# Zero fills on another engine, shorter decay loads, one more order condition and a new order table in a gated-recurrence plus feed-forward kernel

## The chip, the cores and the metric

The kernel runs on one core of a Trainium2 chip. The metric is the device time of one execution in microseconds (us), the median of several runs. The core has TensorE (PE in the profile; PEld is its weight load), VectorE (DVE), ScalarE (ACT), GpSimd (POOL) and SyncE (SP), which here only issues DMA transfers. TensorE's clock has two levels, 1.2 and 2.4 GHz; the profile gives the granted clock as a share of the upper one.

## The reference

Two stages follow each other. The first is a recurrence over 768 time steps for 4 batches of 8 heads of width 40; the second is a feed-forward layer with a rational activation. Weights of the second stage arrive as 64-bit floats.

```python
for t in range(S):                       # S = 768, per batch and head
    m_new = max(f[t] + m, i[t])
    f_stab, i_stab, m = exp(f[t] + m - m_new), exp(i[t] - m_new), m_new
    C = f_stab * C + i_stab * outer(v[t], k[t])
    n = f_stab * n + i_stab * k[t]
    y[t] = sigmoid(o_gate[t]) * (C @ q[t]) / max(abs(n @ q[t]), 1)
x = y as (3072, 320)
h = x @ w_in                             # 320 -> 2048
g = (a0 + a1*h + a2*h*h + a3*h**3) / (1 + |b0|*|h| + |b1|*h*h + 1e-6)
out = g @ w_out                          # 2048 -> 320
```

## The kernel before

The recurrence is computed in chunks of 64 steps. A *unit* u handles 128 steps (two chunks) of one batch with its eight heads: 24 units. A *block* n of the feed-forward layer takes the 256 tokens of units 2n and 2n+1 (tile `xk`), and runs in eight *stages* i, each over 256 of the 2048 hidden columns: 12 blocks, 96 stages.

For a unit, SP loads the keys and queries (`ld`: tiles `kr` and `qn`), the values (`lv`: `vb`), and the gate factors from scratch memory (`lg`: `fb` and `ab`). `ab` holds the cumulated decays, the same row copied to 64 + 64 partitions. Then `kp` scales the keys (POOL), `tk` transposes them (PE, first transposes), `ek` copies them out (ACT), `tq` transposes the queries (PE, second transposes), `eq` copies them out (ACT), `qa` multiplies them with `ab` (DVE), `S` forms the scores (PE), `sc` builds the decay matrix `e` (DVE), `P` and `ke` apply it, `ow` forms the sums that update the state (PE), `u0` and `u1` update the states `sm` and `st` (DVE) with `d0` and `d1` (POOL) before them, `it` and `i1` form the output in PSUM tile `y`, and `ab`, `rc`, `g`, `x`, `xt`, `xh`, `xl` normalise it, gate it and write it transposed into `xk`.

A feed-forward stage is `f1` (PE, PSUM tile `ph`), `ha`, `p1`, `u`, `y`, `r0` on ACT, `p3`, `gh`, `m`, `gl` on DVE, `w` and `rm` on POOL, and `f2`, `f3` on PE (PSUM tile `po`, from `gH` and `gL`). Before that the 64-bit weights are loaded in 18 slabs (`raw`: names j0, j1 for the last 64 rows of `w_in`, i0 to i7 for the rest of it, o0 to o7 for `w_out`) and turned into two 32-bit parts: `s0` (ACT), `s1` (DVE), `s0`, `s1`, `o0` (ACT), `o2` (POOL).

At the start the gate factors of the first two chunks are computed on DVE (`early`, tiles `early_e`, `early_kT`, `early_qA`), stored to scratch, and read back by `lg`; those of all other chunks follow (`gates`). Some tiles must be zero where no load writes them: `kp`, `vb0`, `qn0` and `qb` are cleared before the branch on the flag, and `qn1`, `vb1`, `sm`, the four `st` and half of `wY` in `setup`. PE is given 90 products of the identity (`hot`) to do where nothing else is ready.

The order on each engine is fixed when the kernel is built. Every step is added to a planner with an order key, and the planner takes on each engine, among the steps whose inputs are there, the one with the lowest key. It assumes a cost for each step, and 2.75 us from the end of an issue to the landing of a load. A unit's key is

```python
base = 2 * u - LEAD + (UNIT_AT[u] if u < len(UNIT_AT) else 0.0)
key = base + ATT_AT[name] + LOAD_AT[u]      # LOAD_AT for SP's steps of units 0 to 7
```

and for a weight slab with number `key` in the order j0, i0, o0, i1, o1, j1, i2, o2, i3, o3, ...

```python
at = PREP_AT[op] + PREP_AT["step"] * key + SLAB_AT[key] + (PREP_AT["out"] if name[0] == "o" else 0.0)
```

to which `NUDGE` adds a number of its own for single steps. Each engine then runs its list in order: an instruction that waits holds up all behind it on its engine, SP's list included. A condition in the planner (`r`, `w`) between steps of the same engine fixes their order and is no wait on the chip.

Of the kernel before, what the change touches and what calls it, by code (L numbers as in the profile page):

```python
# [189 lines left out]
BLOCK_AT = (-30.05, -20.9)  # L190
# [11 lines left out]
    o0_i3=-86.73, o2_i3=-68.16, raw_o3=-30.6, s0_o3=-86.83, s1_o3=-112.32, o0_o3=18.04, o2_o3=-97.03,
    raw_i4=-20.87, s0_i4=19.22, s1_i4=-143.2, o0_i4=21.48, o2_i4=-312.68, s0_o4=-160.32, s1_o4=0.96, o0_o4=3.24,
    raw_i5=-8.26, s0_i5=-110.61, s1_i5=-96.8, o0_i5=-137.56, o2_i5=-81.65, raw_o5=34.48, s0_o5=-123.6,
    s1_o5=-133.73, o0_o5=25.43, o2_o5=-182.58, raw_i6=-62.5, s0_i6=-109.42, o0_i6=-14.16, o2_i6=-230.79,
    s0_o6=2.67, s1_o6=-71.7, o0_o6=44.51, o2_o6=-403.32, raw_i7=5.23, s0_i7=-13.29, s1_i7=-238.6, o0_i7=39.05,
    o2_i7=-23.84, raw_o7=-36.78, s0_o7=3.25, s1_o7=-198.97, o2_o7=-67.4, ogl_0=-0.03, og_0=3.41, ld_0=-6.33,
    lg_0=11.88, lv_0=12.65, kp_0=100.21, sc_0=50.31, tk_0=915.2, ek_0=-1.35, tq_0=997.06, eq_0=-0.9,
    qa_0=138.15, S_0=40.63, ke_0=-15.75, P_0=11.71, ow_0=914.85, u0_0=-0.64, i1_0=-94.1, u1_0=-5.16,
    rc_0=137.27, g_0=87.1, x_0=113.44, xt_0=949.12, xh_0=106.04, lg_1=201.84, lv_1=181.76, kp_1=123.51,  # L210
    sc_1=-6.49, tk_1=936.74, ek_1=20.81, eq_1=20.85, qa_1=55.87, ke_1=25.86, P_1=179.55, it_1=24.11, u0_1=7.7,
    d1_1=89.23, u1_1=4.5, ab_1=77.75, rc_1=45.19, g_1=-14.56, x_1=-19.25, xt_1=971.3, xh_1=138.71, xl_1=64.48,
    ogl_3=1.48, ogl_4=3.6, ogl_5=1.54, og_2=-50.77, ld_2=139.07, lg_2=182.61, lv_2=-82.51, kp_2=116.69,
    sc_2=99.12, tk_2=909.8, ek_2=123.31, tq_2=991.7, eq_2=118.94, qa_2=34.83, S_2=-21.68, ke_2=-12.55,
    P_2=-1.16, it_2=921.63, u0_2=11.63, d1_2=-128.57, i1_2=-79.84, u1_2=108.87, rc_2=25.69, g_2=-133.39,
    x_2=123.07, xt_2=-44.66, xh_2=-33.5, xl_2=54.23, lg_3=-0.89, lv_3=252.92, kp_3=93.7, sc_3=-10.43,
    tk_3=-65.69, tq_3=15.48, eq_3=0.4, qa_3=152.51, S_3=1.34, ke_3=-23.2, P_3=157.11, ow_3=-66.94, it_3=-56.07,
    u0_3=151.6, d1_3=85.48, i1_3=945.59, u1_3=178.13, g_3=15.21, x_3=146.78, xt_3=41.5, xh_3=197.9,
    xl_3=-210.89, ld_4=112.13, lg_4=157.92, lv_4=117.27, kp_4=101.03, sc_4=136.18, ek_4=144.46, eq_4=-3.95,
    qa_4=-17.72, S_4=-2.95, ke_4=-73.28, P_4=-50.56, d0_4=-6.47, ow_4=-11.6, it_4=-1.13, u0_4=-51.89,  # L220
    d1_4=27.44, i1_4=-0.94, u1_4=22.81, rc_4=-145.43, g_4=71.53, x_4=97.04, xt_4=72.26, xh_4=201.32, xl_4=69.51,
# [1086 lines left out]
```

## Time and profile before

| | |
|---|---|
| median of 3 runs | 573.15 us (570.04 to 574.14) |
| the profiled execution | 573.32 us |
| its span, first to last instruction | 571.4 us |
| around the span | 1.92 us |
| PE, DVE, ACT, POOL busy | 526.4, 475.8, 430.8, 394.3 us |
| mean granted clock of PE | 0.959 |

The profile follows one execution on each engine. Busy time is time in which an engine has an instruction under way, a wait for a memory port included. Idle time before an instruction is put down to what ended it (after `<-`). Helper functions record every instruction of the program at line 34, so tiles name the work.

### The profile page before, as it was taken

To read this page: it belongs to the slowest core of one execution; us is meant where nothing else is said; L and a number is where in the kernel's file an instruction comes from. 1 tells how busy PE (TensorE), PEld (TensorE's weight loads), DVE (VectorE), ACT (ScalarE), POOL (GpSimd) and SP (SyncE) were. 2 spreads that over 40 slices of the span, in tenths; PEclk is the share of its full clock that TensorE was granted. 3 is DMA by queue.
4 is the path that set the end of the run, shared out by engine and by line. 5 is a ranking of instruction groups with operands and counts; after the bars stand their busy time and mean duration, and the time that the engine had idled before them with its cause. 6 is when DMAs were issued, how large, how long until landed. Compare 5 with 4: busy or idle time off the path is not lost.

```text
span 571.4 us, 13096 instructions
## 1 busy us (share of the span) xinstructions
PE 526.4 (92%) x5024; PEld 492.9 (86%) x5024; DVE 475.8 (83%) x782; ACT 430.8 (75%) x757; POOL 394.3 (69%) x353
## 2 busy tenths in 40 slices
PE   4956796899999999999999999999999999999994
PEld 4955676799989999999999898899899999999993
DVE  8979898997888779987888877877987878878684
ACT  2647689886866888777788868888877777778982
POOL 4536669996687697777868684586777686757762
PEclk9967597999999999999999999999999999999998
DMA  5799877422331323333313214232122010000000
GB/s 168 173 241 243 227 171 157 89 62 58 91 67 45 64 50 77 65 72 77 78 38 85 36 50 97 64 66 73 35 64 70 13 36 2 1 26 1 23 1 30
DMA packets 120666, 44.10 MB, mean 77 GB/s; under 512 B 103826, under 2 KB 113106, under 8 KB 120594
## 3 DMA queue, kind: packets, MB, share of 16 engines
q1 hardware_dynamic: 120594, 43.18, 33.2%
q8 instruction: 41, 0.67, 0.5%
q14 instruction: 31, 0.25, 0.1%
HBM read 39.03 MB, written 4.13 MB: 76 GB/s over the span
## 4 chain that ended last, share of the span: by engine, by line
PE 68%; DVE 11%; POOL 6%; issue 4%; DMA 3%; ACT 3%; SPq 3%; DVEq 0%; POOLq 0%; ACTq 0%
PE ph L34 27%; PE po L34 25%; PE y L34 6%; PE ps L34 4%; PE kq L34 3%; PE ow L34 2%; DVE w L34 2%; DVE gH L34 2%; POOL p L34 2%; DVE gL L34 1%; ACT ph L34 1%; POOL tm L34 1%; PE px L34 1%; DMA rawj<-in_moe_w_in_dram 1%; DMA rawo<-in_moe_w_out_dram 1%
## 5 line engine op out<-in xcount | busy, mean ns | idle before, releaser
L34 POOL TENSOR_TENSOR p<-p,w 128x512 f32<-128x512 f32 (+1 forms) x97 | 128.7, 1327 | 85.0 <-DVE w L34 78.3
L34 PE MATMUL ph<-xk,wi 128*128 128x256 f32 x1152 | 173.8, 286 | 0.9 <-DVE gL L34 0.7
L34 POOL TENSOR_TENSOR w<-w,ha 128x512 f32<-128x512 f32 (+1 forms) x97 | 138.4, 1427 | 34.9 <-ACT w L34 31.0
L34 PEld LDWEIGHTS ph<-xk,wi 128*128 128x128 f32 x1152 | 151.9, 188 | 5.9 <-issue 1.9
L34 PE MATMUL po<-wo,gH 128*128 128x320 f32 x768 | 135.8, 315 | 1.8 <-DVE gH L34 1.8
L34 PEld LDWEIGHTS po<-wo,gH 128*128 128x128 f32 x768 | 114.9, 188 | 4.8 <-DVE gH L34 2.6
L34 DVE SCALAR_TENSOR_TENSOR gH<-p,ps,ph 128x512 fp32r<-128x512 f32 (+1 forms) x97 | 71.6, 738 | 34.0 <-PE po L34 15.3
L34 DVE SCALAR_TENSOR_TENSOR w<-w,gH 128x512 f32<-128x512 f32 (+1 forms) x97 | 84.3, 870 | 5.7 <-POOL p L34 0.5
L34 ACT ACTIVATE ha<-ph 128x512 f32<-128x512 f32 (+1 forms) x97 | 57.4, 592 | 40.6 <-PE ph L34 40.4
L34 ACT ACTIVATE w<-ha,ba 128x512 f32<-128x512 f32 (+1 forms) x97 | 78.7, 811 | 4.8 <-POOL p L34 0.4
L34 ACT ACTIVATE ph<-w,cd 128x512 f32<-128x512 f32 (+1 forms) x97 | 66.2, 683 | 20.3 <-DVE p L34 14.4
L34 PE MATMUL po<-wo,gL 128*128 128x320 f32 x384 | 77.1, 318 | 4.3 <-DVE gL L34 4.0
L34 DVE SCALAR_TENSOR_TENSOR gL<-p,ps,ph 128x512 fp32r<-128x512 f32 (+1 forms) x97 | 71.3, 735 | 10.4 <-POOL p L34 8.8
L34 DVE SCALAR_TENSOR_TENSOR p<-p,ps,ph 128x512 f32<-128x512 f32 (+1 forms) x97 | 71.0, 736 | 4.3 <-ACT p L34 3.4
L34 PEld LDWEIGHTS po<-wo,gL 128*128 128x128 f32 x384 | 59.3, 188 | 8.3 <-DVE gL L34 6.5
L34 ACT ACTIVATE p<-ph,ps 128x512 f32<-128x512 f32 (+1 forms) x97 | 65.4, 674 | 0.9 <-DVE gL L34 0.7
L34 ACT ACTIVATE ph<-ph 128x512 f32<-128x512 f32 (+1 forms) x97 | 56.1, 579 | 2.7
L34 PE MATMUL ph<-xk,wj 128*128 128x256 f32 x192 | 54.1, 282 | 0.0
L34 PE MATMUL ph<-xk,wY 128*128 128x256 f32 x192 | 53.8, 280 | 0.0
L34 DVE TENSOR_TENSOR_SCAN e<-fb,eye 128x512 f32<-128x512 f32 x24 | 37.0, 1542 | 0.2
L34 PEld LDWEIGHTS ph<-xk,wY 128*128 128x128 f32 x192 | 36.2, 189 | 0.0
L34 PEld LDWEIGHTS ph<-xk,wj 128*128 128x128 f32 x192 | 36.2, 189 | 0.0
(127 smaller groups left out, 781.7 us busy)
## 6 DMA issues: line engine op xcount, KB each, us to landing
fb<-scrF SPq DMA_DIRECT2D x48, 128.0 KB, 3.1
ab<-scrA SPq DMA_DIRECT2D x48, 128.0 KB, 3.3
rawo<-in_moe_w_out_dram SPq DMA_DIRECT2D x8, 640.0 KB, 6.3
rawi<-in_moe_w_in_dram SPq DMA_DIRECT2D x8, 512.0 KB, 6.7
og<-in_o_gate_dram SPq DMA_DIRECT2D x24, 160.0 KB, 3.4
...
```

What stands on the lines that cost most here:

```text
L34: made = fn(*args, **kwargs)
```

## The change

The fills that `setup` made on POOL are made on ACT, as copies of the zero tile `kp`, 512 columns at most in one instruction; POOL keeps the two small fills with ones in `vb1`. The three buffers of `ab` become tiles of their own that are cleared once, and a load of `ab` writes 40 + 40 rows in place of 64 + 64; `lg` is told to come after the clearing. `tq` of a unit comes after `ow` of the unit before it. All order tables of the branch that the inputs take, `NUDGE` with some 700 numbers among them, are new.

```diff
 ATT_AT = dict(
-    lg=-59.2, ogl=-10.05, lv=-18.58, ld=-15.11, og=3.91, kp=-104.14, tk=5.17, tq=-78.71, sc=6.82, ek=-27.18,
+    lg=-3.83, ogl=-22.75, lv=30.2, ld=5.45, og=4.73, kp=-56.39, tk=0.91, tq=-146.46, sc=-5.07, ek=-48.3,
...
-PREP_AT = dict(step=5.78, out=6.38, raw=-10.83, s0=-2.2, s1=30.22, o0=5.52, o2=28.86)
+PREP_AT = dict(step=4.73, out=4.24, raw=3.21, s0=2.49, s1=40.29, o0=-10.57, o2=0.17)
 SLAB_AT = (
-    -43.3, 8.83, -36.5, -14.88, 25.7, -11.49, -34.84, -23.78, -5.52, -9.83, 1.9, -6.29, -36.2, -25.85, 6.51,
+    -22.43, 48.08, -29.62, -34.02, 30.04, -1.82, 24.33, -21.49, -71.36, 82.88, 20.89, -43.02, 3.52, -19.75,
...
-LOAD_AT = (25.22, -118.48, -94.28, -111.54, 28.04, 48.32, -127.63, -111.81)
-LEAD = -2.42
-UNIT_AT = (-13.8, -38.23, -26.17, -51.88, -49.08, -26.82)
+LOAD_AT = (76.66, 26.09, -15.52, -13.06, -14.84, -11.42, 76.63, 19.27)
+LEAD = -1.14
+UNIT_AT = (-24.19, -49.27, -25.94, -28.68, -28.28, -52.95)
...
 NUDGE = dict(
+    raw_j0=5.09, s0_j0=-234.95, s1_j0=-53.37, o0_j0=143.57, o2_j0=30.46, raw_i0=-49.78, s0_i0=18.31,
...
+    s0_o1=-149.58, s1_o1=-222.82, o0_o1=-8.02, o2_o1=26.85, raw_j1=-55.12, s0_j1=-376.0, s1_j1=-79.04,
...
+    o0_i3=-55.64, o2_i3=-127.99, raw_o3=60.02, s0_o3=567.76, s1_o3=-0.12, o0_o3=-375.43, o2_o3=-362.16,
...
+    s0_o7=-45.88, s1_o7=-524.01, o0_o7=-57.44, o2_o7=-292.79, ogl_0=-20.83, ogl_1=-17.81, og_0=-237.59,
+    ld_0=-70.85, lg_0=-73.59, lv_0=-88.97, kp_0=2.27, sc_0=23.69, tk_0=-181.08, ek_0=-124.2, tq_0=1174.19,
...
+    abs_ = [cp.tile([P, 2, NP, L], F32, name=f"ab{j}") for j in range(3)]
...
-        def clear(engine, t):
-            engine.memset(t, 0.0)
-            if t is vb[1]:
-                ones(engine, t)
+        zeros = common["kp"].rearrange("p h t -> p (h t)")
+
+        def fill(t):
+            names = " ".join("abcd"[: len(t.shape) - 1])
+            t = t.rearrange(f"p {names} -> p ({names})")
+            n, w = t.shape
+            for a in range(0, w, H * L):
+                nc.scalar.copy(t[:, a : min(a + H * L, w)], zeros[0:n, 0 : min(H * L, w - a)])
+
+        def fill_y():
+            for a in range(0, DFF, H * L):
+                nc.scalar.copy(wY[L:P, a : a + H * L], zeros[L:P])
...
-        later = [("qn1", qn[1], 0.5), ("vb1", vb[1], 0.8), ("sm", sm, 0.3)]
-        later += [(f"st{j}", t, 0.3) for j, t in enumerate(st)]
+        later = [("qn1", qn[1], 0.6), ("vb1", vb[1], 0.85), ("sm", sm, 0.45)]
+        later += [(f"z{j}", t, 0.5) for j, t in enumerate(abs_)]
+        later += [(f"st{j}", t, 0.45) for j, t in enumerate(st)]
...
-            plan.add("zero", FIRST, "POOL", cost, lambda t=t: clear(nc.gpsimd, t), w=names)
-        plan.add(
-            "zero", FIRST, "POOL", 2.0, lambda: nc.gpsimd.memset(wY[L:P].bitcast(F32), 0.0), w=["wj0", "wj1"]
-        )
+            plan.add("zero", FIRST - 1, "ACT", cost, lambda t=t: fill(t), w=names)
+        plan.add("zero", FIRST - 1, "ACT", 1.8, fill_y, w=["wj0", "wj1"])
+        plan.add("zero", FIRST, "POOL", 0.25, lambda: ones(nc.gpsimd, vb[1]), w=["vb1"])
...
-            d["ab"] = ap2.tile([P, 2, NP, L], F32, tag="ab", name=f"ab{u}")
+            d["ab"] = abs_[turn[0] % 3]
+            turn[0] += 1
...
-                r = slice(c * L, (c + 1) * L)
+                r = slice(c * L, c * L + D)
...
-                    .unsqueeze(0).broadcast_to([L, 2, NP * L]),
+                    .unsqueeze(0).broadcast_to([D, 2, NP * L]),
...
-        add("lg", "SP", 1.9, lg, r=scr, w=["fb", "ab"], lag=plan.DMA, new=[("fb", ("fb", BUFS["fb"])), ("ab", ("ab", 3))])
+        add("lg", "SP", 1.9, lg, r=[*scr, f"=z{u % 3}"], w=["fb", "ab"], lag=plan.DMA, new=[("fb", ("fb", BUFS["fb"])), ("ab", ("ab", 3))])
...
-        add("tq", "PE", 0.43, f_tq, r=[Q, "kT"], w=["kq"], new=[("kq", ("a", 1))])
+        add("tq", "PE", 0.43, f_tq, r=[Q, "kT", "=odone"], w=["kq"], new=[("kq", ("a", 1))])
...
-        add("ow", "PE", 0.85, f_ow, r=["pm.1", V], w=["ow"], new=new("ow", "a", 1))
+        add("ow", "PE", 0.85, f_ow, r=["pm.1", V], w=["ow", "=odone"], new=new("ow", "a", 1))
```

## Rows read from the trace of the kernel before

**Rows 1.** The page's first part: busy time of each engine, its share of the span and its instructions.

```profile
PE 526.4 (92%) x5024; PEld 492.9 (86%) x5024; DVE 475.8 (83%) x782; ACT 430.8 (75%) x757; POOL 394.3 (69%) x353
```

**Rows 2.** Busy time by stretch: from and to, length, then for each engine busy us (instructions), the granted clock of PE, the mean busy share of the 16 DMA engines, and GB/s.

```profile
0.00:14.30 14.30, 6.88 (x32) 6.52 (x33) 11.48 (x41) 2.94 (x5) 6.83 (x19) 0.95 0.57 168
14.30:28.60 14.30, 13.42 (x111) 13.22 (x110) 14.19 (x18) 8.75 (x14) 7.81 (x7) 0.93 0.74 173
28.60:71.40 42.80, 28.49 (x244) 24.64 (x246) 37.12 (x60) 27.12 (x55) 24.49 (x21) 0.64 1.04 237
71.40:128.60 57.20, 48.99 (x528) 44.27 (x525) 52.99 (x86) 49.26 (x87) 48.62 (x40) 0.94 0.54 120
...
143.00:550.00 407.00, 401.38 (x3878) 379.76 (x3878) 335.83 (x542) 324.19 (x566) 288.11 (x252) 1.00 0.23 51
550.00:571.40 21.40, 12.86 (x83) 11.29 (x81) 13.10 (x20) 9.61 (x19) 9.07 (x9) 0.87 0.06 20
```

**Rows 3.** The chain of work that ended last, in order of time, from 5.74 us: start us, us, what (SPq is SP's queue of DMA issues).

```profile
5.74 1.33 DVE early_kT L34
7.09 1.84 DVE early_kT L34
...
12.74 4.02 DMA scrF<-early_kT
...
31.66 6.07 DMA rawj<-in_moe_w_in_dram
37.80 0.65 ACT rawj L34
38.45 0.47 ACT kT L34
```

**Rows 4.** The tile `early_kT`, its instructions by kind: count, duration in ns (least, median, greatest), first and last start in us, shapes.

```profile
L34 DVE TENSOR_SCALAR early_kT<-early_kT x3: 210/1316/1829, 5.7 to 11.6; 64x128 f32<-64x128 f32 x2, 64x128 int32<-64x128 int32 x1
L34 DVE TENSOR_SCALAR early_qA<-early_kT x2: 218/218/219, 9.0 to 9.8; 64x128 f32<-64x128 f32 x2
```

**Rows 5.** POOL in order of time from 5.68 us: start us, us, what, count, and in brackets the idle time before it.

```profile
5.68 1.30 POOL L34 MEMSET st<- 104x328 f32 x4
7.04 1.80 POOL L34 MEMSET wY<- 64x2048 f32 x1
15.88 3.73 POOL L34 TENSOR_TENSOR gate_w<-gate_i,gate_m 32x192 f32<-32x192 f32 x4 [7.04 <-DMA scrA<-early_qA]
```

**Rows 6.** ACT in order of time, its first two instructions, and four casts in a row at 24.55 us.

```profile
9.45 1.28 ACT L34 ACT_TABLE_LOAD   x1 [9.45 <-DMA rawj<-in_moe_w_in_dram]
10.75 0.67 ACT L34 ACTIVATE rawj<-rawj 128x512 int32<-128x512 uint8 x1
...
24.55 2.55 ACT L34 CAST wj<-zj 64x512 fp32r<-64x512 f32 x4 [1.76 <-DVE zj L34]
```

**Rows 7.** ACT's groups with shapes kept apart: busy us, mean ns of one, idle time before.

```profile
L34 ACT CAST wi<-zi 128x512 fp32r<-128x512 f32 x8 | 4.9, 618 | 2.2 <-DVE zi L34 2.1
L34 ACT ACTIVATE ot<-po,pa 128x320 f32<-128x320 f32 x23 | 12.0, 526 | 5.5 <-PE po L34 5.2
```

**Rows 8.** SP's issues in order of time: start us, us that the queue was taken, line, transfer, count.

```profile
4.18 1.21 SPq L720 DMA_DIRECT2D rawj<-in_moe_w_in_dram  x2
5.43 0.58 SPq L578 DMA_DIRECT2D gate_f<-in_f_gate_dram  x1
...
7.46 0.94 SPq L720 DMA_DIRECT2D rawi<-in_moe_w_in_dram  x2
...
16.83 1.10 SPq L837 DMA_DIRECT2D fb<-scrF  x2
18.03 1.30 SPq L843 DMA_DIRECT2D ab<-scrA  x2
19.38 0.59 SPq L1077 DMA_DIRECT2D og<-in_o_gate_dram  x1
...
24.17 0.58 SPq L822 DMA_DIRECT2D kr<-in_k_dram  x1
...
30.68 1.57 SPq L720 DMA_DIRECT2D rawj<-in_moe_w_in_dram  x2
...
79.88 0.58 SPq L720 DMA_DIRECT2D rawo<-in_moe_w_out_dram  x1
```

**Rows 9.** Who waited for whom in the first 143 us, on ACT and on DVE: total us, times, longest.

```profile
ACT rawj L34 <- DMA rawj<-in_moe_w_in_dram: 7.4, 1, 7.4
DVE rawj L34 <- ACT rawj L34: 2.6, 1, 2.6
```

**Rows 10.** DMA issues from 28.6 to 71.4 us: transfer, count, KB each, median us from issue to landing.

```profile
ab<-scrA SPq DMA_DIRECT2D x4, 128.0 KB, 5.9
```

**Rows 11.** PE in order of time, the sums `ow` and the second transposes (`kq<-ident,qn`) of the first units.

```profile
45.00 0.77 PE L34 MATMUL ow<-vb,pm 128*40 128x82 f32 x16 [0.46 <-DMA vb<-in_v_dram]
...
56.97 1.10 PE L34 MATMUL kq<-ident,qn 128*104 128x128 f32 x4
```

**Rows 12.** PE in order of time: the first products from `xk` (`f1` of stage 0 of block 0) and those from `gH` (`f2`) of its stage 3.

```profile
76.35 0.98 PE L34 MATMUL ph<-xk,wi 128*128 128x256 f32 x6
...
118.79 1.34 PE L34 MATMUL po<-wo,gH 128*128 128x320 f32 x8
```

**Rows 13.** POOL in order of time: the last low part (`o2`) of a `w_out` slab.

```profile
115.37 1.56 POOL L34 TENSOR_TENSOR wo<-zo,wo 128x640 fp32r<-128x640 f32 x1
```

More of the change, by code (lines that the diff above doesn't have):

```diff
@@ L202 @@
[L202 to L221, printed above, removed]
@@ new lines @@
+    w_1_2=93.76, y_1_2=288.33, r0_1_2=221.97, gh_1_2=-265.16, m_1_2=157.36, rm_1_2=197.81, gl_1_2=-482.37,
+    f2_1_2=0.13, f3_1_2=294.03, f1_1_3=-5.24, ha_1_3=-25.91, p1_1_3=4.83, p3_1_3=-22.02, w_1_3=201.12,
+    y_1_3=276.4, r0_1_3=339.22, gh_1_3=-267.53, m_1_3=168.21, gl_1_3=-63.54, f2_1_3=-2.26, f3_1_3=291.19,
+    f1_1_4=-5.71, ha_1_4=-154.2, p1_1_4=-350.57, p3_1_4=-92.55, w_1_4=0.11, y_1_4=387.09, r0_1_4=338.75,
+    gh_1_4=3.47, m_1_4=308.58, rm_1_4=185.62, gl_1_4=-5.7, f2_1_4=30.57, f3_1_4=292.85, f1_1_5=0.67,
@@ new lines @@
+    ha_1_5=-30.82, p1_1_5=-1.86, p3_1_5=-93.08, u_1_5=-0.96, y_1_5=286.8, r0_1_5=292.16, gh_1_5=141.39,
+    m_1_5=160.91, rm_1_5=-1.05, f3_1_5=323.49, f1_1_6=0.2, ha_1_6=-48.11, p1_1_6=9.47, p3_1_6=-238.99,
+    u_1_6=19.0, w_1_6=-0.53, y_1_6=228.81, r0_1_6=51.45, gh_1_6=-0.67, m_1_6=310.11, rm_1_6=-1.55,
+    gl_1_6=-213.75, f2_1_6=-0.99, f3_1_6=238.71, f1_1_7=2.65, ha_1_7=-326.24, p1_1_7=-289.51, p3_1_7=-35.62,
+    u_1_7=-271.21, w_1_7=-1.5, y_1_7=284.69, r0_1_7=348.65, gh_1_7=0.89, m_1_7=320.21, rm_1_7=138.58,
@@ new lines @@
+    gh_2_5=213.39, rm_2_5=1.29, gl_2_5=-212.25, f2_2_5=-1.06, f3_2_5=307.1, ha_2_6=-398.34, p1_2_6=3.71,
+    p3_2_6=-29.99, u_2_6=22.99, w_2_6=108.7, r0_2_6=345.06, gh_2_6=-199.49, m_2_6=-38.83, rm_2_6=0.77,
+    gl_2_6=-404.74, f2_2_6=13.2, f3_2_6=0.42, f1_2_7=-86.97, ha_2_7=-32.05, p1_2_7=2.66, p3_2_7=-442.87,
+    u_2_7=26.23, w_2_7=0.88, y_2_7=-86.58, r0_2_7=0.97, gh_2_7=78.37, m_2_7=156.93, gl_2_7=-405.02,
+    f2_2_7=-293.53, f3_2_7=291.57, ev_2_7=0.88, f1_3_0=-0.56, ha_3_0=-30.59, u_3_0=26.8, w_3_0=9.41,
@@ L283 @@
+    y_3_0=-62.38, gh_3_0=-156.98, m_3_0=156.4, f1_3_1=-1.14, p1_3_1=-340.05, p3_3_1=-165.37, u_3_1=-8.55,
+    w_3_1=-0.1, y_3_1=-63.43, gh_3_1=194.69, m_3_1=117.16, f1_3_2=12.95, u_3_2=56.39,
+)
+GATE_AT = -39.89
+HOT_AT = 129.25
 COLD = 0
-STORE_AT = 85.52
+STORE_AT = 112.32
 START = dict(DVE=4.1, ACT=4.0, POOL=3.6, PE=4.1, SP=3.8)
@@ L1089, in gates_o @@
         plan.add(f"og_{u}", key + ATT_AT["og"], "ACT", 2.6 + 0.36 * many, act, w=[f"og{w}" for w in units])
-    OG, xk = {}, {}
+    OG, xk, turn = {}, {}, [0]
     PO = {}
```

156 lines of the change are left out of this document (84 added, 72 removed).

## Prediction

> **What bounds the kernel now.** I read the busy times first. PE is busy 92% of the span [rows 1], so the question is where the other 8% lies, and the table by stretch tells it. From 143 to 550 us PE is idle 407.00 − 401.38 = 5.6 us; the last 21.4 us hold 8.5 us of idle time [rows 2]. That is the steady part and the tail: together 14 us, and the change adds nothing to either but another order. The start is different. By 128.6 us PE shows 6.88 + 13.42 + 28.49 + 48.99 = 97.8 us of busy time, and much of that is the `hot` products and work at a granted clock of 0.64 (between the two levels of 1.2 and 2.4 GHz). Meanwhile DVE is busy 14.19 of 14.30, 37.12 of 42.80 and 52.99 of 57.20 us [rows 2]. So in the start DVE, fed by loads, is the bound, and after it PE is. From 28.6 to 71.4 us the DMA engines are full as well (share 1.04, 237 GB/s). What the change is worth is decided before about 130 us.
>
> Then the chain of waits. It runs through DVE's early gate work, through the store to scratch and its landing at 12.74 + 4.02 = 16.76 us, through SP's queue, which reads it back at 16.83 us, and through the transfer `rawj` issued at 31.66 us, which ACT waits for until 37.80 us, with the copy `kT` of unit 0 right behind it [rows 3, 8].
>
> **The change, part by part.** The sum is made against the profiled execution, 573.3 us (span 571.4 and 1.9 around it), which is 0.2 us above the median of the three runs.
>
> *Fills leave POOL.* Two DVE instructions of the early chain take 1316 and 1829 ns, while the same operation on the same shape takes 218 ns a moment later [rows 4]. They start at 5.74 and 7.09 us, under POOL's fills of `st` and `wY`, and the second ends at 8.93 us, when the fill of `wY` ends (7.04 + 1.80 = 8.84 us) [rows 3, 5]. The fills hold DVE up: 1316 + 1829 − 2 × 218 = 2.7 us, on the chain, with SP waiting behind it for the store. Without them the store goes at 12.74 − 2.7 = 10.0 us. POOL's own time is worth nothing here, since it then sits idle 7.04 us [rows 5]. Term: **−2.7 us**, ends −2.7 and 0. The Trainium skill, SBUF — State Buffer, section Who interferes with whom, calls the port pair of DVE and GpSimd an exclusive lock that a one-input DVE instruction in a 2-port mode waits for; the rows agree, with 1829 ns against 218.
>
> *Fills arrive on ACT.* 15 copies: nine of 512 columns (`qn1` 1, `vb1` 1, `ab` 3, `wY` 4), five of 328, one of 144. By the nearest rows 9 × 0.618 + 6 × 0.526 = 8.7 us [rows 7]; four casts in a row take 2.55 us [rows 6], more than 4 × 0.618, so I count no overlap. ACT is idle until 9.45 us and then loads a table for 1.28 us [rows 6], so from 4.0 us the fills end at 12.7 and that load near 14.0 us in place of 10.73: 3.3 us late for the first weight steps. Behind the fills stand `s0` of the first slabs and the copy of the early factors, which the scaling of unit 0's keys needs, after 18 us (below). ACT's idle time from 14.3 to 28.6 us, 5.5 us [rows 2], 1.76 of them before the casts of `wj` [rows 6], takes the delay up. Term: **0**; if DVE found nothing else to do meanwhile, +3.3. `lg`'s new condition stands on SP with the whole queue behind it; it ends with the fills by 12.7 us, before the data it loads is there (14 us, below). `kp`'s first write and `qn1`'s first load, which the fills must precede, come after 18 us. All three cost nothing as long as the fills end by 14 us; past that SP loses what they take longer.
>
> *Decay loads of 40 + 40 rows.* 48 KB less in each of 48 loads. Four fall between 28.6 and 71.4 us [rows 10], 0.19 MB, 0.8 us at 237 GB/s [rows 2]. Elsewhere the DMA share is 0.27 to 0.74 and nothing is gained. Ends −0.8 and 0, **−0.4**. The Trainium skill (DMA: Bandwidth & Descriptors, Why a DMA increments its semaphore by 16 and not by 1) says that a transfer is spread over the largest number of engines up to 16 that divides its slowest dimension: 40 rows would go over 10 engines with four rows each, as 64 go over 16 with four each. By that the fullest engine carries what it did, and the term would be 0, the sum 0.4 us higher. No run so far shows a 40-row load.
>
> *`tq` after the sums.* In the trace `ow` of unit 0 is at 45.00 us and `tq` of unit 1 at 56.97 [rows 11], so the order already held there. Both are on PE, so no wait is added; where it binds, all PE work queued behind `tq` shifts with it. **0**.
>
> *New order.* Here one reads keys. For SP the tables give, in the new order: `ogl` 0 and 4 (−42.4), gates (−39.9), `ogl` 3 (−39.9), i1 (−39.8), `ogl` 1, 2, 5 (−38 to −39), j1 (3.21 + 5 × 4.73 − 1.82 − 55.12 = −30.1), `lg` 0 (−23.8), j0 (3.21 − 22.43 + 5.09 = −14.1), and `ld` 0 (1.14 − 24.19 + 5.45 + 76.66 − 70.85 = −11.8). All but `lg` can go at once; the stores go as soon as they are ready. By the times of single issues [rows 8], from 4.18 us three `ogl` (3 × 0.59), the gate loads (5.43 to 7.46, 2.0 us) and i1 (0.47) are over at about 8.4 us, then SP waits until 10.0. After it three store issues (taken at 0.58 each), three `ogl` (1.8 us), j1 (1.2), `lg` 0 (1.10 + 1.30; ready at 10.0 + 4.0) and j0 (1.2): keys of unit 0 at 18.3 us, not 24.17 [rows 8], 5.9 us sooner, of which 2.7 are already counted.
>
> More important is which slab is in the way. In the old order j1 came after the keys, at 30.68 us [rows 8], and ACT stood 7.4 us for it, with DVE idle 2.6 us [rows 9]. In the new one j1 and j0 come before the keys, so this wait goes. It is worth at least DVE's 2.6 us and at most ACT's 7.4; I take **−4.5**, below the middle, since DVE is the fuller engine. What is late next is another slab under the same full DMA stretch, or DVE itself. The steady order can move PE's 5.6 us of idle time either way: 0.
>
> Sum: −2.7 + 0 − 0.4 + 0 − 4.5 = −7.6, so 573.3 − 7.6 = **565.7 us**.
>
> **The rivals.** *Little happens* (571 us): DVE's 115.8 us of work by 128.6 us have to be done whatever comes first, ACT's 3.3 us come through, and gaps that close at 35 us open again at 60, so only the fills' 2.7 us are left. For: DVE's busy share. Against: DVE is idle 10 us between 14.3 and 128.6 us [rows 2], so there is something to close. That the change doesn't do what it says, DVE being held by other POOL work at the same place, belongs here: 573 us.
>
> *Slower* (581 us): slab o3. Its new key is 3.21 + 9 × 4.73 + 82.88 + 4.24 + 60.02 = 192.9, the highest of all slabs, so it is loaded last, and its first ACT step carries a nudge of 567.76. Stages are summed in order in `po`, so stage 3 waits for it and with it stages 4 to 7; `gH` has two buffers and `ph` four banks, so PE can run only a little ahead. In the old trace the last slab is issued at 79.88 us and its low part is done at 115.37 + 1.56 = 116.9 us [rows 8, 13], while stage 3's products begin at 118.79 [rows 12]. If o3 takes this path 10 us more slowly than that last slab did, PE loses about 10 − (118.8 − 116.9) = 8 us plus the gain of the other steps: 573.3 + 8 = 581. It decides from the moment o3 is ready later than stage 3 is otherwise due, about 111 us when the rest gains 7.6. Against it: between 71.4 and 128.6 us ACT is idle 8 us, so the steps of one slab find room.
>
> *More* (557 us): all of DVE's 10 us of idle time in the start close, with the fills 12.7, and some of PE's 5.6 us later: 573.3 − 12.7 − 3.6 = 557.
>
> **How the numbers follow.** Chances: forecast 0.42 (561 to 569), little happens 0.26 (569 to 575), slower 0.18 (576 to 585), more 0.14 (553 to 561). Runs of this kernel spread over 0.7%, so about 1%, 567.4 or 578.9 us, is what can be told from no change. Faster by over 1%: 0.14 and most of the forecast's 0.42 (0.36 of it lies below 567.4), 0.50; slower: 0.17 of the slow case's 0.18; the same: the remaining 0.33. The range leaves out the upper half of the slow case and the lower half of the fastest: 555 to 580. It takes in the unknown costs, +3.3 for ACT and 0 for the loads.
>
> **What would show it.** The two `early_kT` instructions at about 218 ns and the store issued near 10 us; 15 copies on ACT from 4 us on, and its first weight step at 13 to 14 us; the keys of unit 0 issued near 18 us with both rawj before them; no wait of ACT for `rawj` over 2 us; the first products from `xk` (76.35 us before [rows 12]) some 5 to 10 us sooner, and the stretch that PE fills from 128.6 us on beginning near 121. The decay loads should land no later than before. The prediction is wrong if DVE's idle time before 130 us stays at 10 us, if stage 3 of block 0 waits for o3, or if PE's idle time from 143 to 550 us moves by more than its 5.6 us.

## The result, and the profile after

The changed kernel takes 574.91 us (median of 17 runs, 573.45 to 576.62) against 571.31 us for the kernel before, run beside it (17 runs, 570.04 to 574.77): ratio 1.0065, 95% interval 1.0052 to 1.0077. The forecast was 565.7 us, faster; measured is 0.65% slower, clear of noise by its interval, though within the 1% that I called no change. That it lies inside the range of 555 to 580 us is owed to the width of the range, which took in the rivals, and not to the reasoning behind the forecast. The profiled execution of the changed kernel has a span of 574.2 us (571.4 before).

Busy time by stretch, columns as in [rows 2]:

```profile
14.30:28.60 14.30, 8.50 (x61) 8.29 (x60) 10.72 (x16) 8.42 (x19) 5.97 (x7) 0.83 0.97 191
28.60:71.40 42.80, 26.62 (x284) 23.05 (x282) 40.80 (x64) 28.22 (x54) 27.46 (x20) 0.70 0.84 225
71.40:128.60 57.20, 46.57 (x489) 42.24 (x486) 54.27 (x75) 44.37 (x81) 45.00 (x37) 0.94 0.46 107
...
143.00:550.00 407.00, 401.56 (x3930) 379.25 (x3929) 341.27 (x550) 322.71 (x564) 284.90 (x253) 1.00 0.22 50
550.00:574.20 24.20, 15.17 (x101) 13.60 (x99) 14.30 (x22) 11.89 (x23) 10.55 (x10) 0.91 0.06 18
```

The steady part has not moved: PE is idle 5.4 us from 143 to 550 us, 5.6 before, and 14.5 us from 143 us to the end, 14.2 before. But from 143 us on it still has 401.56 + 15.17 = 416.7 us of work, where the kernel before had 414.2 [rows 2]. These 2.5 us are nearly all of the 2.8 us between the two spans, so the loss is made before 143 us, where DVE is the bound. From 71.4 to 128.6 us PE is busy 2.4 us less than in [rows 2] at the same granted clock of 0.94, while DVE is busy 1.3 us more (54.27 for 52.99), with 75 instructions where it did 86. Fewer instructions in more busy time is the thing to explain.

What the first 25 us show of the predicted steps. DVE, the two instructions of the early chain that took 3.2 us in [rows 3, 4]; then ACT in order of time; then SP's issues:

```profile
5.74 0.47 DVE L34 TENSOR_SCALAR early_kT<-early_kT 64x128 f32<-64x128 f32 x2
```

```profile
3.84 1.28 ACT L34 ACT_TABLE_LOAD   x1 [3.84 <-DVE flag_out L388]
5.14 0.62 ACT L34 COPY qn<-kp 128x512 f32<-128x512 f32 x1
...
12.74 0.67 ACT L34 ACTIVATE rawi<-rawi 128x512 int32<-128x512 uint8 x1 [0.68 <-DMA rawi<-in_moe_w_in_dram]
...
18.09 0.69 ACT L34 ACTIVATE rawj<-rawj 128x512 int32<-128x512 uint8 x1 [1.97 <-DMA rawj<-in_moe_w_in_dram]
```

```profile
9.07 3.37 SPq L1104 DMA_DIRECT2D og<-in_o_gate_dram  x3
12.49 1.28 SPq L746 DMA_DIRECT2D rawj<-in_moe_w_in_dram  x2
13.88 0.52 SPq L546 DMA_DIRECT2D scrF<-early_kT  x1
...
18.29 1.09 SPq L864 DMA_DIRECT2D fb<-scrF  x2
...
20.39 0.64 SPq L848 DMA_DIRECT2D kr<-in_k_dram  x1
```

The port lock is gone, ACT's first weight step comes at 12.74 us, both `rawj` are issued ahead of unit 0's keys, and ACT's wait for `rawj` is 2.0 us instead of 7.4 [rows 9]. The store to scratch is late, 13.88 us, although its data are ready at 10.0, and unit 0's keys go at 20.39 us, where I had said 18.3.

### The profile page after: what moved, and what is told of

It reads as the page before. It is cut to its first block, busy times and chain, and to the rows that moved or that the text cites. A ratio compares the mean times of both kernels' runs of the same rounds, so it can differ in the third digit from the quotient of the medians.

```text
span 574.2 us, 13083 instructions
## 1 busy us (share of the span) xinstructions
PE 522.0 (91%) x5024; PEld 488.9 (85%) x5024; DVE 482.2 (84%) x782; ACT 437.5 (76%) x772; POOL 387.5 (67%) x345
## 4 chain that ended last, share of the span: by engine, by line
PE 71%; DVE 13%; issue 5%; DMA 3%; ACT 3%; SPq 3%; POOL 1%; DVEq 0%; POOLq 0%; ACTq 0%
PE ph L34 27%; PE po L34 26%; PE y L34 6%; PE kq L34 4%; PE ps L34 3%; PE ow L34 3%; DVE w L34 2%; DMA rawo<-in_moe_w_out_dram 2%; DVE gH L34 2%; ACT ph L34 2%; DVE gL L34 1%; SPq L746 1%; DVE p L34 1%; PE px L34 1%; PE hot L34 1%
## 5 line engine op out<-in xcount | busy, mean ns | idle before, releaser
L34 POOL TENSOR_TENSOR w<-w,ha 128x512 f32<-128x512 f32 (+1 forms) x97 | 135.9, 1402 | 31.1 <-ACT w L34 29.5
L34 DVE SCALAR_TENSOR_TENSOR w<-w,gH 128x512 f32<-128x512 f32 (+1 forms) x97 | 85.6, 882 | 4.6
L34 DVE SCALAR_TENSOR_TENSOR gL<-p,ps,ph 128x512 fp32r<-128x512 f32 (+1 forms) x97 | 71.1, 733 | 13.2 <-POOL p L34 11.7
L34 PE MATMUL po<-wo,gL 128*128 128x320 f32 x384 | 75.9, 317 | 5.2 <-DVE gL L34 5.1
L34 DVE TENSOR_TENSOR_SCAN e<-fb,eye 128x512 f32<-128x512 f32 x24 | 44.3, 1846 | 3.2 <-DMA fb<-scrF 3.0
L34 PEld LDWEIGHTS y<-vb,pm 128*64 128x64 f32 x768 | 25.2, 141 | 17.4 <-ACT wo L34 13.4
L34 PE MATMUL y<-vb,pm 128*64 128x41 f32 x768 | 27.8, 234 | 13.3 <-DVE xn L34 13.3
```

The costliest lines, as they stand in the source:

```text
L34: made = fn(*args, **kwargs)
```

## The experiments

Each set of kernels ran beside the kernel before, whose median was 571.0 to 572.2 us in them, so the ratios are what is compared; a kernel has 5 to 17 runs. b_lite, a_lite and a_memset leave out a part of the work on the weights and are no kernels to use.

| kernel | median us | ratio to before, 95% interval |
|---|---|---|
| changed kernel | 574.91 | 1.0065 (1.0052 to 1.0077) |
| b_fills | 571.67 | 0.9999 (0.9982 to 1.0015) |
| b_fills_rows | 570.42 | 0.9987 (0.9969 to 1.0005) |
| a_order_only | 578.54 | 1.0122 (1.0101 to 1.0144) |
| a_rows64 | 576.32 | 1.0089 (1.0069 to 1.0109) |
| a_pool_fills | 575.65 | 1.0079 (1.0050 to 1.0107) |
| b_stores_first | 571.72 | 1.0004 (0.9984 to 1.0023) |
| a_tail | 576.96 | 1.0092 (1.0060 to 1.0124) |
| a_late | 574.30 | 1.0050 (1.0031 to 1.0068) |
| a_tail_late | 577.38 | 1.0104 (1.0073 to 1.0135) |
| b_lite | 568.47 | 0.9938 (0.9915 to 0.9961) |
| a_lite | 564.99 | 0.9891 (0.9872 to 0.9909) |
| a_memset | 567.41 | 0.9940 (0.9914 to 0.9965) |
| a_low_dve | 572.33 | 1.0017 (1.0003 to 1.0031) |
| a_low_dve6 | 571.69 | 0.9994 (0.9978 to 1.0010) |
| b_rawj1_low_dve | 572.59 | 1.0017 (0.9993 to 1.0041) |
| b_only_rawj1 | 571.15 | 0.9986 (0.9964 to 1.0008) |
| b_rawj1_early | 568.30 | 0.9955 (0.9934 to 0.9976) |
| b_rawj1_again | 568.27 | 0.9936 (0.9914 to 0.9958) |

Names with b_ start from the kernel before, with a_ from the changed one. Unless said otherwise the order of every engine's list is kept; "X ahead of Y" means that X alone is moved in its engine's list.

### The parts, one at a time

**b_fills**: the kernel before, fills emitted on ScalarE at the same place of the order.

```diff
-            engine.memset(t, 0.0)
+            fill(t)
...
-lambda: nc.gpsimd.memset(wY[L:P].bitcast(F32), 0.0)
+fill_y
```

> The kernel before, with nothing changed but the engine of the fills: the same fills as copies of zeros on ScalarE, the order of all other work kept. Theory (the fills are a gain, and it is the new order that lost it): both early_kT instructions at 218 ns, the scrF store issued near 10.0 us since nothing stands ahead of it on SP in this order, unit 0's keys about 2.7 us sooner; 568.6 to 569.8 us against 571.3, ratio 0.995 to 0.998. Rival A (DVE's sum of work sets the start, gaps reopen): the same 218 ns, but 571.3 within 0.6. Rival B (15 copies on ScalarE delay its first weight steps by 3 us and that comes through): 573 or more.

**b_fills_rows**: b_fills, and

```diff
-                r = slice(c * L, (c + 1) * L)
+                r = slice(c * L, c * L + D)
...
-                    .unsqueeze(0).broadcast_to([L, 2, NP * L]),
+                    .unsqueeze(0).broadcast_to([D, 2, NP * L]),
```

> The kernel before, with fills on ScalarE and decay loads of 40 + 40 rows into three fixed buffers cleared on ScalarE (three more copies), order kept. This is all of the change but the order and the condition on tq. Theory: b_fills less 0 to 0.8 us, so 567.8 to 569.8. Rival A: 571.3 within 0.6. Rival C (the 40-row loads cost something, being spread over other engines or landing later): over b_fills by 1 us or more.

**a_pool_fills**: the changed kernel, fills back on GpSimd.

```diff
-                nc.scalar.copy(t[:, a : min(a + H * L, w)], zeros[0:n, 0 : min(H * L, w - a)])
+                nc.gpsimd.memset(t, 0.0)
```

> The changed kernel in its own order, with all fills back on GpSimd (memsets). The two early_kT instructions go back to 1.3 and 1.8 us or so. Theory (in this order SP wouldn't pass the gain on, since its store stands behind three og loads and rawj1 and went at 13.88 us, where the data were ready at 10.0): 574.9 within 0.8, the store within 0.5 us of 13.9. Rival D (the fills' gain was in the changed kernel too): 577.6. Rival B (copies on ScalarE cost what they delay): 572 to 573.

**a_order_only**: a_pool_fills with `broadcast_to([L, ...])` and 64-row slices again, and **a_rows64**: the changed kernel with those rows alone.

> The changed kernel in its own order, with fills on GpSimd and decay loads of 64 + 64 rows: the order is all that is left of the change. Theory (the order is what costs): 574.5 to 576, ratio to the kernel before 1.005 to 1.009. Rival (order neutral, fills or loads cost): 571.3 within 0.8.

> The changed kernel with decay loads of 64 + 64 rows in place of 40 + 40 and nothing else. The rows were worth 2.9 us in this order with the fills on GpSimd (578.5 and 575.65) and 1.2 us in the old one (571.7 and 570.4). Theory (the loads of the start set its pace, eight of these loads are issued before 50 us, 0.38 MB less at 225 to 237 GB/s is 1.6 us): 576 to 577.5. The prediction's price was 0.4: 575.3. By the rule of the Trainium skill (DMA: Bandwidth & Descriptors, Why a DMA increments its semaphore by 16 and not by 1) it would be 574.9.

What follows. The new order alone (with its conditions, and with the three clears of `ab`, which are on GpSimd here) costs 1.22%, 7 us, more than the 0.5 to 0.9% that I expected. In it the fills on ScalarE give back 0.1 to 0.3% (1.0079 to 1.0065 with 40 rows, which by the intervals could be nothing, and 1.0122 to 1.0089 with 64) and the rows 0.24% (1.0089 to 1.0065) to 0.43% (1.0122 to 1.0079), 1.4 to 2.5 us. In the old order the fills give nothing (0.9999), and the rows 0.12%, which is not told from zero. So no part but the order is seen to cost anything, and the order is the loss: 0.78%, 4.5 us, from b_fills_rows to the changed kernel.

### Where the fills' 2.7 us went

In b_fills the lock is gone and the copies have come, both at once. The copies did not eat the gain: ScalarE's table load for the gates `og` starts at 26.11 us there and at 27.76 before. Nothing stands ahead of the store on SP. Its issues, then one of the kernel before, and below the transfers issued from 4 to 20 us with count, KB and median us from issue to landing, first of b_fills, then of the kernel before:

```profile
8.50 0.47 SPq L733 DMA_DIRECT2D rawo<-in_moe_w_out_dram  x1
10.10 0.48 SPq L528 DMA_DIRECT2D scrF<-early_kT  x1
...
16.11 1.57 SPq L850 DMA_DIRECT2D fb<-scrF  x2
```

```profile
8.45 0.48 SPq L720 DMA_DIRECT2D rawo<-in_moe_w_out_dram  x1
```

```profile
rawo<-in_moe_w_out_dram SPq DMA_DIRECT2D x1, 640.0 KB, 7.4
...
scrF<-early_kT SPq DMA_DIRECT2D x1, 16.0 KB, 5.9
```

```profile
rawo<-in_moe_w_out_dram SPq DMA_DIRECT2D x1, 640.0 KB, 8.1
...
scrF<-early_kT SPq DMA_DIRECT2D x1, 16.0 KB, 4.0
```

The store goes 2.64 us sooner (10.10 for 12.74) and lands 0.7 us sooner (16.0 for 16.7): 16 KB take 5.9 us instead of 4.0, and both times they land just behind the 640 KB of `rawo` (8.50 + 7.4 = 15.9; 8.45 + 8.1 = 16.6). **b_stores_first** puts two of those slabs behind it:

```diff
+MOVES = [("raw_i2", "raw_i1"), ("raw_o0", "raw_i1")]   # on top of b_fills_rows
```

> b_fills_rows with two loads moved on SP: raw_i2 and raw_o0 are issued behind the stores of the early factors instead of ahead of them. In b_fills the store went 2.6 us sooner than before (10.10 for 12.74 us) but landed only 0.7 us sooner (16.04 for 16.77), right behind raw_o0 (15.87). Theory (transfers of the full DMA engines land in the order of issue, so the store waits for the slabs ahead of it): the store lands near 13.2 us, fb of unit 0 is issued at 13 to 13.5 us (15.43 in b_fills_rows, 16.83 before), and the time falls by 0.5 to 2.5 us against b_fills_rows: 568 to 570, ratio to before 0.994 to 0.998. Rival A (the start is bound by the sum of loads and of DVE's work, not by when unit 0 begins): fb as early, but 570.4 within 0.8. Rival F (the store's round trip is slow for itself): it lands 5 us or more after its issue again.

Its store and the load that reads it back, and DVE's wait for `rawo` in b_stores_first and in b_fills_rows:

```profile
10.05 0.48 SPq L565 DMA_DIRECT2D scrF<-early_kT  x1
...
13.56 1.21 SPq L890 DMA_DIRECT2D fb<-scrF  x2
```

```profile
DVE rawo L34 <- ACT rawo L34: 3.7, 2, 3.5
```

```profile
DVE rawo L34 <- ACT rawo L34: 1.3, 2, 1.1
```

The store, issued at 10.05 us again, has landed by 13.56: what it waited for was the slabs issued ahead of it. But unit 0's decays, 1.9 us sooner than in b_fills_rows, gave no time either (1.0004 against 0.9987). DVE now waits 3.7 us for the slab that was moved, 1.3 us in b_fills_rows, so the gain at one place came back as a wait at another; what the earlier decays are worth by themselves, no run shows. In the changed kernel the store is held on SP instead, by three `og` issues that took 3.37 us and one `rawj`.

### Repairing the new order by its waits

In the changed kernel unit 0's sums `ow` run at 29.29 us, 15.7 us sooner than in [rows 11], and then unit 0 stops. PE's two longest waits from 40 to 130 us, and DVE and POOL at the second of them:

```profile
PE y L34 <- DVE xn L34: 13.3, 1, 13.3
PE y L34 <- DVE sm L34: 4.3, 1, 4.3
```

```profile
81.84 0.48 DVE L34 TENSOR_TENSOR xn<-y,gt 128x320 f32<-128x320 f32 x1
82.24 5.73 DVE L34 TENSOR_TENSOR_SCAN e<-fb,eye 128x512 f32<-128x512 f32 x1
87.89 0.72 DVE L34 SCALAR_TENSOR_TENSOR p<-p,ps,ph 128x512 f32<-128x512 f32 x1
```

```profile
81.88 0.73 POOL L34 TENSOR_TENSOR tm<-sm,ab 104x328 f32<-104x328 f32 x1
82.57 1.28 POOL L34 TENSOR_TENSOR w<-w,ha 128x512 f32<-128x512 f32 x1
83.81 3.07 POOL L34 TENSOR_TENSOR wo<-zo,wo 128x640 fp32r<-128x640 f32 x2
90.91 0.74 POOL L34 TENSOR_TENSOR tm<-sm,ab 104x328 f32<-104x328 f32 x1 [4.03 <-DVE sm L34]
```

The scan, 1.21 us at its least, ends 1.1 us after POOL's last instruction does (86.88). My first theory was that these two waits were the loss. **a_tail** removes the first, **a_late** the second, **a_tail_late** both:

```diff
+MOVES = [   # a_tail
+    ("rc_0", "s1_i0"), ("g_0", "o2_i0"), ("qa_1", "s1_i2"), ("x_0", "s1_i5"), ("u0_1", "s1_o4"),
+    ("d1_1", "o2_i0"), ("xh_0", "s0_o5"), ("xl_0", "sc_2"), ("u1_1", "sc_2"), ("ab_1", "o0_o2"),
+    ("rc_1", "s1_o2#2"), ("g_1", "o2_i5"), ("x_1", "s1_i6"),
+]
+MOVES = [("o2_o5", "rm_0_0"), ("o2_o6", "rm_0_0")]   # a_late
```

> The changed kernel with 13 steps of units 0 and 1 (the normaliser, gating and transposes of unit 0, the state update, query scaling and normaliser of unit 1) moved up on DVE, GpSimd and ScalarE to where their data are ready; the rest of every engine's order is kept. In the changed kernel ab_0 is done at 44.7 us, but rc_0 stands on DVE behind weight steps until 53.0, x_0 until 58.5, and PE waits 13.3 us for it. Theory (what the new order wins at unit 0 is lost in the lists of DVE and GpSimd): PE's wait before unit 1's second product falls below 4 us, the load of og_7, which waits for g of an early unit, goes before 58 us (61.2 now), the first FFN product comes 3 to 7 us before 74.6, and the time falls by 2.5 to 5 us: 570 to 572.5. Rival A (DVE's 117 us of work by 128.6 us set the end whatever stands first): PE's wait falls as much, but the time stays at 574.9 within 0.8.

> The changed kernel with two GpSimd steps moved: the low parts of slabs o5 and o6 (o2_o5, o2_o6) stand behind ke_4 instead of ahead of d1_3 and ke_4. Theory (DVE's scan for unit 4, 5.73 us at 82.24 in place of 1.2, is held out of the memory by four GpSimd instructions in a row, which end at 86.88): the scan falls to 2.5 us or less, PE's 4.3 us wait for DVE sm at 86.5 falls below 2, and the time falls by 1.5 to 2.7 us: 572.2 to 573.4. Rival A: the scan is short, but 574.9 within 0.8. Rival E (the scan is slow for another reason, its own inputs): the scan stays over 4 us.

> Both moves together. Theory: the two losses lie one after the other, so the sum of both, 4 to 7.5 us less than 574.9: 567.5 to 571. Rival A: 574.9 within 0.8. If the second only appears because of where the first leaves GpSimd, no more than a_tail alone.

PE's waits in a_tail, and DVE and POOL in a_late:

```profile
PE pi L34 <- ACT kT L34: 9.3, 1, 9.3
PE y L34 <- DVE pm L34: 4.2, 1, 4.2
```

```profile
81.90 1.46 DVE L34 TENSOR_TENSOR_SCAN e<-fb,eye 128x512 f32<-128x512 f32 x1
...
88.13 3.20 DVE L34 SCALAR_TENSOR_TENSOR w<-w,gH 128x512 f32<-128x512 f32 x1
```

```profile
87.73 3.06 POOL L34 TENSOR_TENSOR wo<-zo,wo 128x640 fp32r<-128x640 f32 x2
```

The theory fell. In a_tail the 13.3 us become 4.2, but another wait of 9.3 us comes behind it, so PE's wait was moved and not removed, and the time is no better (1.0092, and 1.0104 with both moves). In a_late the scan falls to 1.46 us, so the moved GpSimd work had held it, but the two low parts now lie on `w`, which takes 3.20 us (0.71 in the changed kernel), and of the gain 0.15% is left, which the intervals do not tell from nothing. The loss went with GpSimd's instructions to what DVE did beside them.

### GpSimd's weight work

Which of DVE's instructions suffer shows in its groups from 14.3 to 128.6 us, changed kernel first, then the kernel before (count, busy us, mean ns, idle before):

```profile
L34 DVE TENSOR_TENSOR_SCAN e<-fb,eye 128x512 f32<-128x512 f32 x7 | 16.4, 2342 | 3.1 <-DMA fb<-scrF 3.0
L34 DVE SCALAR_TENSOR_TENSOR zi<-zi,rawi 128x512 int32<-128x512 int32 x8 | 9.2, 1161 | 0.0
...
L34 DVE SCALAR_TENSOR_TENSOR p<-p,ps,ph 128x512 f32<-128x512 f32 x7 | 5.0, 731 | 0.1
```

```profile
L34 DVE TENSOR_TENSOR_SCAN e<-fb,eye 128x512 f32<-128x512 f32 x7 | 10.5, 1493 | 0.1
...
L34 DVE SCALAR_TENSOR_TENSOR zi<-zi,rawi 128x512 int32<-128x512 int32 x8 | 6.7, 832 | 0.0
L34 DVE SCALAR_TENSOR_TENSOR p<-p,ps,ph 128x512 f32<-128x512 f32 x8 | 5.9, 734 | 0.0
```

Instructions with both operands in SBUF (`e`, `zi`) are slower by 0.85 and 0.33 us each; `p`, with an operand in PSUM, keeps its 0.73 us in both. Two groups alone are 16.4 − 10.5 + 9.2 − 6.7 = 8.4 us, of which other groups give some back (`rawi` is the faster in the changed kernel, 758 ns for 1148). Over all groups, what DVE's instructions that start in this stretch take beyond the least of their kind (same operation, tiles and shape) in any run adds up to 30.3 us in the changed kernel and 25.0 before, while DVE's idle time falls from 10.0 to 8.5 us. Together that is 3.8 us more, near the 2.8 us between the spans. In a_order_only, one execution as well, the two are 25.6 and 12.9 us: its loss stands in idle time and not in longer instructions. So the second theory, for the changed kernel: the new order lays GpSimd's work on DVE's two-operand instructions. **b_lite** (on b_fills_rows) and **a_lite** (on the changed kernel) take most of that work away; **a_memset** fills GpSimd's time again without reading:

```diff
-            lambda t, z: subtract(t[:, n : 2 * n], z, t[:, 0:n]),
+            lambda t, z: subtract(t[:, n : n + n // 8], z[:, 0 : n // 8], t[:, 0 : n // 8]),
...
+        for _ in range(2):   # a_memset alone
+            nc.gpsimd.memset(t[:, n + n // 8 : 2 * n].bitcast(F32), 0.0)
```

> b_fills_rows with seven eighths of the GpSimd work on the weights left out: the low part of each i and o slab is computed for the first eighth of its columns only, and the products take the high part twice instead, so that PE's work is the same (the output is not the reference's). 12.6 us or so of GpSimd's 20 steps of 1.2 to 1.5 us before 120 us go. Paired with a_lite, which is the same in the changed order. Theory G (the new order costs what it does because GpSimd's work comes to lie on DVE's instructions with two operands in SBUF, which take 8.1 us over their least between 71.4 and 85 us in the changed kernel and 2.5 in b_fills_rows): without that work the two orders come together, a_lite over b_lite by 1.5 us at most, where after stands 4.5 us over b_fills_rows (574.9 and 570.4). Rival H (the new order costs by its lists, its waits or its steady part): a_lite over b_lite by 3.5 us or more. b_lite itself: 566 to 569.

> The changed kernel with the same seven eighths of the GpSimd weight work left out and the high part taken twice. Theory G: within 1.5 us of b_lite, 566 to 570. Rival H: 3.5 us or more over it, 570 to 573.

> a_lite with GpSimd's time filled up again: behind each cut low part (first eighth of the columns) GpSimd clears the rest of the low half twice, so that it is as long busy as in the changed kernel, but reads no second operand meanwhile (the output is not the reference's, as in a_lite). Theory G (what costs is GpSimd reading while DVE's instructions with two SBUF operands run; in the early gate work DVE's instructions with two operands kept their 0.2 to 0.28 us beside clears): DVE's scan at 82 us under 2.5 us, 565 to 568.5. Rival I (what a_lite won is GpSimd's own time, its list being the bound): 573 to 575.5.

The scan `e` in the changed kernel and in a_memset (count, ns least, median, greatest); in a_memset two of DVE's instructions with both operands in SBUF, and what POOL did beside the first and beside the second; and PE's longest wait in a_lite:

```profile
L34 DVE TENSOR_TENSOR_SCAN e<-fb,eye x24: 1211/1485/5726, 22.7 to 486.0; 128x512 f32<-128x512 f32 x24
```

```profile
L34 DVE TENSOR_TENSOR_SCAN e<-fb,eye x24: 1184/1250/2317, 22.0 to 482.5; 128x512 f32<-128x512 f32 x24
```

```profile
57.29 0.68 DVE L34 SCALAR_TENSOR_TENSOR zi<-zi,rawi 128x512 int32<-128x512 int32 x1
...
83.48 3.79 DVE L34 SCALAR_TENSOR_TENSOR zo<-zo,rawo 128x640 int32<-128x640 int32 x1
```

```profile
57.04 1.00 POOL L34 MEMSET wi<- 128x448 f32 x2
```

```profile
82.92 1.23 POOL L34 TENSOR_TENSOR pm<-kp,e 128x320 f32<-128x320 f32 x1
84.11 1.25 POOL L34 TENSOR_TENSOR p<-p,w 128x512 f32<-128x512 f32 x1
85.33 1.25 POOL L34 TENSOR_TENSOR w<-w,ha 128x512 f32<-128x512 f32 x1
```

```profile
PE y L34 <- DVE xn L34: 12.5, 1, 12.5
```

Without the low parts the new order is the faster one, 0.9891 against 0.9938, which is further than theory G had it; with them it is the slower one, 1.0065 against 0.9987. They cost 0.5% in the old order and 1.7%, 9.9 us, in the new. With GpSimd kept busy by clears (1.00 us for the pair on an `i` slab; 76.6 us from 14.3 to 128.6 us, 78.4 in the changed kernel and 67.9 in a_lite) 1.25% of the 1.74% stay won, 7.1 of the 9.9 us: most of the cost is GpSimd's reading beside DVE, not the time in its list. The trace of a_memset is of one of its longer runs, 571.85 us, where the nine go from 566.04 to 571.95. Wholly beside clears `zi` takes 0.68 us; `zo` at 83.48 us, beside `pm`, `p` and `w` of GpSimd, which read, takes 3.79. The rest, 0.5%, is GpSimd's time or the clears' own effect; no run parts these. And a_lite still has the 12.5 us wait of PE and is the fastest kernel of all, so that wait is not what makes the new order the slower one. The Trainium skill (SBUF — State Buffer, Who interferes with whom) says that a DVE instruction with two SBUF inputs contends with a GpSimd instruction that reads SBUF and not with one that only writes it; these runs agree, and 5.73 us for 1.21 is the number.

**a_low_dve**, **a_low_dve6** and **b_rawj1_low_dve** leave nothing out, but let DVE do the low parts at the same place of the order (all 16, six, all 16):

```diff
-            lambda t, z: subtract(t[:, n : 2 * n], z, t[:, 0:n]),
+            lambda t, z: on.tensor_tensor(t[:, n : 2 * n], z, t[:, 0:n].bitcast(F32), op=ALU.subtract),
...
+        on = nc.vector if name in ("o4", "i5", "o2", "o1", "o5", "o6") else nc.gpsimd   # a_low_dve6
```

> The changed kernel with the low parts of the i and o slabs subtracted by DVE at the same place of the order instead of GpSimd; nothing left out. It costs DVE 8 x 0.65 and 8 x 0.81 = 11.7 us and saves it up to what a_lite saved, 16.8 us of instructions over their least by 130 us. Theory G: 568 to 573, ratio below after's. Rival (DVE's own list is already full, 11.7 us more come through): 580 or more.

> The changed kernel with six low parts subtracted by DVE instead of GpSimd, those beside which DVE lost most: o4, i5, o2, o1, o5, o6. Nothing is left out. It costs DVE 5 x 0.81 + 0.65 = 4.7 us and saves what stands beside these six in the changed kernel, 1.0 (rawo at 54.8) + 2.2 (zi at 58.9) + 1.9 (zi at 72.3, scan at 73.4) + 3.1 (of the scan at 82.2) = 8.2 us. Theory G: 3.5 us less than 574.9, 570 to 572.5. Rival (the loss moves to the next instruction, as it mostly did in a_late): 574 to 575.

> b_rawj1_early with the same low parts on DVE. In that order DVE's instructions are 19.8 us over their least by 130 us, some 10 of them beside low parts, and DVE is idle for 5 us; 11.7 us of work come to it. Theory G: no gain, 568 to 573. If contention cost more than it shows, below 567.

Giving DVE, the bound, six more instructions (5.9 us in its trace, where I had 4.7) makes the changed kernel 0.7% faster (1.0065 to 0.9994), as expected; all sixteen, 14.9 us in the trace and not 11.7, still 0.5%. In the old order, where less is lost, the same move costs (0.9936 to 0.9955 becomes 1.0017). So the price is in the pairing that an order happens to make.

### The one load

My −4.5 us was for `rawj1` coming sooner. **b_rawj1_early** makes that step alone on b_fills_rows, **b_only_rawj1** on the kernel before, and **b_rawj1_again** is b_rawj1_early a second time.

```diff
+MOVES = [("raw_j1", "lg_0")]
```

> b_fills_rows with one load moved on SP: raw_j1 is issued ahead of lg_0 instead of behind the og loads. That is the step that I priced at 4.5 us by ScalarE's wait of 7.4 us and DVE's of 2.6 us on rawj. Prediction's step: both waits go, 566 to 568. Theory (the DMA engines are full until 60 us and land in the order of issue, so one load sooner is the others later, and DVE's work sets the end): the wait on rawj falls below 2 us, others take its place, 570.4 within 0.8.

> The kernel before with one load moved: raw_j1 ahead of the decay load of unit 0 on SP; fills, rows and all other order as before. b_rawj1_early stood 2.1 us below b_fills_rows (568.3, 570.4) and had next to no idle time on DVE from 17 to 88 us. Theory (that gain belongs to the one load): 568.5 to 570, ratio 0.995 to 0.998. Rival (it needs the fills and rows): 571 within 0.8.

> b_rawj1_early a second time, beside other runs, since one load alone gave 0.8 us (b_only_rawj1, 571.15) and with fills and rows 3.1 (568.3, seven runs). If the three add up (fills 0, rows 0.7 to 1.3, load 0.8): 569 to 570.3. If they need each other: 568.3 within 0.7 again.

DVE's wait for `rawj` in b_fills_rows, and the stretch from 28.6 to 71.4 us there, in b_rawj1_again and in b_only_rawj1:

```profile
DVE rawj L34 <- ACT rawj L34: 1.9, 1, 1.9
```

```profile
28.60:71.40 42.80, 31.48 (x286) 26.80 (x285) 37.52 (x62) 28.02 (x57) 22.50 (x19) 0.61 0.95 232
```

```profile
28.60:71.40 42.80, 28.23 (x296) 23.42 (x296) 40.74 (x67) 30.36 (x61) 25.14 (x22) 0.72 0.96 235
```

```profile
28.60:71.40 42.80, 27.81 (x289) 23.00 (x289) 41.12 (x66) 31.09 (x63) 25.72 (x21) 0.72 1.04 241
```

My theory here (no gain) was wrong: it is 0.3 to 0.5%, 1.8 to 2.9 us, on top of b_fills_rows, and the kernel is below both, 0.45 and 0.64% under the kernel before. DVE is 3.2 us busier in that stretch and does five more instructions; its wait is gone. On the kernel before, where DVE's wait of 2.6 us [rows 9] goes as well and DVE is 4.0 us busier in the stretch, the load gave only 0.14%, with an interval that takes in zero. So the idle time that closes on DVE is no sure price either; whether the load needs the fills and rows, or the sets just differ, stays open.

## Why the prediction was wrong

**What bounds the kernel**: right. PE's idle time from 143 to 550 us stayed (5.4 for 5.6), and it was DVE before 130 us that decided. But three of my signs did not come: DVE's idle time from 14.3 to 128.6 us fell from 10.0 to 8.5 us only, unit 0's keys went at 20.39 us and not near 18, and the first products from `xk` start at 74.55 us, 1.8 us sooner and not 5 to 10.

**The lock, −2.7**: the mechanism was right (218 ns each, early chain done at 10.0), its worth wrong: 0.0 (b_fills, fills and copies together). The step that failed is that a store at 10.0 us has its data there at 14: I carried the 4.02 us of [rows 3] over as if they belonged to the store, though the issues of [rows 8] ahead of it said that it was the last of a queue of slabs. In the changed order the store was late on SP besides, since I took 0.59 us for each `og` issue and one took 2.23.

**Fills on ScalarE, 0**: right as far as the runs go. The first weight step came at 12.74 us, and moving the fills cost nothing in either order; no run has the copies without the end of the lock.

**Rows, −0.4**: too small in the new order, where they gave 1.4 to 2.5 us; the 0.12% (0.7 us) of the old order is not told from zero or from 0.4. I counted only the loads of one stretch; eight are issued before 50 us, all while the DMA engines are near full, which makes 0.38 MB and 1.6 us. SP also takes 0.4 us less for each pair (last section), and no run parts the two. The result of 0 that I gave by the Trainium skill (DMA: Bandwidth & Descriptors, Why a DMA increments its semaphore by 16 and not by 1) is not borne out in the new order; over how many engines the 40 rows go no run here shows.

**`tq` after the sums, 0**: not tried by itself; no run parts it from the new order.

**New order, −4.5**: the step that failed. Measured is +4.5 us (0.78%, from b_fills_rows to the changed kernel). Its mechanism exists: the wait on `rawj` fell as told, the same load moved by itself is worth 1.8 to 2.9 us on b_fills_rows (0.8 us, not told from zero, on the kernel before), near my lower bound, DVE's 2.6 us (ScalarE's 7.4 us were no price), and without GpSimd's low parts the new order is 0.47%, 2.7 us, faster than the old. What I left out is that a new order changes how long instructions last. I took DVE's work to 128.6 us, 115.8 us, as given, while the same instruction lasts 0.71 or 3.20 us by what GpSimd does beside it. The low parts cost 9.9 us in the new order against 2.8 in the old, 7.1 us or 1.2% more, which is more than everything else together. By a_memset 7.1 of the 9.9 are reading beside DVE; how the 2.8 of the old order part, no run shows. I had met the lock in the early chain and did not ask where else it would fall.

**The rivals.** "Little happens" had the time (569 to 575), and rightly that gaps closing early need not carry through (b_stores_first, b_only_rawj1), but not the reason for the loss. "Slower" was the right sign by the wrong place: o3's low part ends at 119.85 us and stage 3 begins at 120.21 with no idle time of PE before it. "More" did not happen.
